# Turned keys with the heads innermost, and a verdict formed by a matmul

## Chip, cores and metric

The kernel runs on one core of a Trainium2 chip. The metric is the device time of one execution in microseconds, taken over several runs; a profile of one further execution shows where the time lies. Engine names in the profile: PE is TensorE's matmul side, PEld its weight loads, DVE is VectorE, ACT is ScalarE, POOL is GpSimd, SP is SyncE. A `q` behind a name means the engine's instruction queue.

## The reference

Two blocks follow each other. The first is a gated linear recurrence over time, with a complex decay per head and channel; the second a dense layer with the activation h cos(h).

```
B, H, S, D = 4, 8, 768, 48
mag   = sqrt(a_re^2 + a_im^2)
scale = min(mag, 0.999) / (mag + 1e-6)         # a_n = a * scale, complex
for t in range(S):                             # per batch and head
    state = a_n[t][:, None] * state + outer(k[t], v[t])     # D x D, complex
    y[t]  = q[t] @ real(state)
x   = y.transpose(0, 2, 1, 3).reshape(3072, 384)
h   = x @ w_in                                 # 384 x 2048
out = (h * cos(h)) @ w_out                     # 2048 x 384
```

q, k, v and a are float32; the two weight matrices come as float64.

## The kernel before, in words

**Two paths.** `fast_path` computes everything in a form that is exact enough for ordinary inputs and gathers measures of whether they were ordinary: `least` (1 where a decay product stayed large enough, 0 where not), `odd` (positive where an input was outside the supported range) and `wide` (sums of squares of h). At the end `verdict` turns them into one flag, every engine reads it, and a branch either runs `general_path`, which computes all again, or, in the other arm, only issues the last store. With these inputs the second arm runs.

**Chunks and groups.** Time is cut into chunks of C = 128 steps: N = 24 chunks, six to a batch. Two chunks make a group; there are NG = 12 groups g. For a chunk the recurrence becomes matmuls: scores of keys against queries (`f_scores`, products `sc`), masked by the causal matrix (tile `atm`), times values (`f_out`, products `yp`), plus the queries times the state carried over (`state`); the next state comes from keys times values (`state_sums`, products `sp`). Keys and queries carry cosine and sine parts, so a head has D2 = 96 rows.

**The dense layer.** `mm1_sums` makes h for a group in eight tiles `hp` (six products each of 128 x 256), which share three PSUM buffers. `gate_sine` takes cosine and square on ScalarE, `gate_product` multiplies on VectorE, which also frees the `hp` buffer. From group 2 on (PLAIN = 2) the second product is done by seven half-size products (`seventh`, products `sum` and `op`) with mixed operands (`mixed`, tiles `s`), in the order p = 0, 1, 3, 2, 5, 4, 6. Each result is scaled by ScalarE or added by VectorE into output tiles `ot`, which SP stores. In the last group the piece c12 lives in the tile `rest`; p = 6 adds to it at the very end, and ScalarE issues its store in the branch's other arm (`late["store"]`).

**Keys and queries turned.** `sc` needs keys and queries with the 96 channels on the partitions. For groups 0 and 1 TensorE turns them (`f_turn`). From group 2 on (PEG = 2) `f_transpose` does it with VectorE and DMAs: VectorE transposes 32 x 32 blocks from `ks` or `qs` into `tr` (128 partitions; 3 blocks, 16 heads, 32 columns), SP moves `tr` to the DRAM tile `moved`, and from there into `kT` or `qT`. For queries this is one DMA in pieces of 2 KB (16 heads of 32 words). For keys it is four DMAs, one per quarter q4 of the chunk's time, in pieces of 128 B, which puts the 128 time steps of a head next to each other in `kT`. Keys are the stationary operand `lhsT` of `sc` (line 965), queries the moving one; `queries` (line 952) hands queries over as four runs of 32 words.

**Order.** Up to group 1 the order of instructions is written out by hand. From group 2 on, `weave` (line 1213) sorts the steps of a stage by a position between 0 and 1 that each list is given, and issues them in that order; each engine takes its own in turn. In a stage n the key and query steps of group n+1 stand at 0.53 to 0.64, between the last half products of group n-1 and the `hp` sums of group n (0.56 to 1.0); `sc` of group n+1 opens the next stage. `behind` and `chain` pin the order of two instructions on an engine without a wait.

**The end.** A last weave takes the seven half products of the last group from 0 to 1, and three steps of `verdict` (line 1608) among them: its first part at 0.1, where the three measures are reduced on VectorE to `low` (96 values) and `even` (128 values); two DMAs write these into a line `line_d` in DRAM and a third brings the line back onto one partition; its second part at 0.59, where VectorE takes the minimum of the line (`bad`) and compares (`flag`), and the engines' reads of the flag are issued, ScalarE's behind its last scaling (`late["scalar"]`); its third at 0.78, which places TensorE's read. VectorE's read stands ahead of the last addition.

Of the kernel before, what the change touches and what calls it, by code (L numbers as in the profile page):

```python
# [11 lines left out]
F32 = mybir.dt.float32  # L12
# [7 lines left out]
ALU = mybir.AluOpType  # L20
AX = mybir.AxisListType
# [466 lines left out]
def fast_path(ctx, tc, q, k, v, a_re, a_im, moe_w_in, moe_w_out, out, least, odd, wide,  # L488
# [7 lines left out]
    nc = tc.nc  # L496
    B, H, S, D = q.shape
    DM, DF = moe_w_in.shape
    C = 128
    NCH = S // C  # L500
    G = 2
    N = B * NCH
    NG = N // G
    D2 = 2 * D
    HH = H // 2
    ND = DM // C
    Q4 = C // 32
    NB = D2 // 32
# [7 lines left out]
    ft = ctx.enter_context(tc.tile_pool(name="ft", bufs=2))  # L516
# [5 lines left out]
    pa = ctx.enter_context(tc.tile_pool(name="pa", bufs=5, space=PSUM))  # L522
# [20 lines left out]
    def behind(ins, other):  # L543
        tc.add_manual_dep(ins.ins, other.ins.name, mybir.DependencyInfo(
            mybir.DependencyClass.NoSync, mybir.DependencyReason.DATA))
# [140 lines left out]
    def matmul(out, **kw):  # L686
        chain(nc.tensor.matmul(out, **kw), "tensor")  # L687
# [233 lines left out]
    def f_transpose(g, i, n, name):  # L921


        if i == 0:
            X[g][name] = ft.tile([D2, G * H, Q4, 32] if name == "kT" else [D2, Q4, G * H, 32], F32,
                                 tag=name, name=name, bufs=1)
        tr = ft.tile([C, NB, n * H, 32], F32, tag="tr", name="tr")
        turn = vector.transpose(out=tr, in_=X[g][name[0] + "s"][:, ds(i * H, n * H)].rearrange(
            "p x a d -> p x (a d)").rearrange("p x (r b) -> p b x r", b=NB))
        if name == "qT" and "gated" in X[g - 1]:  # L930
            behind(turn, X[g - 1]["gated"])
        moved = rows_d.tile([Q4, D2, n * H, 32], F32, tag="moved", name="moved", bufs=3)
        nc.sync.dma_start(out=moved.rearrange("q (r b) x j -> (q r) b x j", b=NB), in_=tr)
        if name == "kT":
            for q4 in range(Q4):
                nc.sync.dma_start(out=X[g][name][:, ds(i * H, n * H), q4], in_=moved[q4])
        else:
            nc.sync.dma_start(out=X[g][name][:, :, ds(i * H, n * H)],
                              in_=moved.rearrange("q c x j -> c q x j"))

    def f_turn(g, i, name, hh):

# [9 lines left out]
    def queries(n, h):  # L952
        g, i = divmod(n, G)
        if g < PEG:
            return X[g]["qT"][:, i * H + h].rearrange("p q j -> p (q j)")
        return X[g]["qT"][:, :, i * H + h]

    def f_scores(n, hh):
        y = Y[n]
        if hh == 0:  # L960
            y["atm"] = ft.tile([C, H, C], F32, tag="atm", name="atm")
        ps = pa.tile([C, HH, C], F32, tag="a", name="sc")
        for h in range(HH):
            head = hh * HH + h
            matmul(ps[:, h], lhsT=X[n // G]["kT"][:, n % G * H + head],
                   rhs=queries(n, head), start=True, stop=True)
        y["masked"] = vector.tensor_tensor(
            out=y["atm"][:, ts(hh, HH)], in0=ps, in1=causal.unsqueeze(1).to_broadcast([C, HH, C]), op=ALU.mult)
# [191 lines left out]
    def seventh(g, p, part):  # L1160


        x, name = X[g], SEVEN[p]
        if p == 0 and part == 0:
            x["sum"] = pm.tile([C, E2], F32, tag="acc", name="sum", bufs=1)
            x["ot"] = [msb.tile([C, DM], F32, tag="ot", name="ot") for _ in range(G)]

        alone = g == NG - 1 and p == 6
        summed = p in (0, 3, 5, 6) and not alone
        if not summed and part == 0:  # L1170
            x["op"] = pm.tile([C, E2], F32, tag="m", name="op", bufs=2)
        ps = x["sum"] if summed else x["op"]
        for j in range(part * HJ // 2, (part + 1) * HJ // 2):
            matmul(ps, lhsT=left(g, name, j), rhs=right[name][:, j],
                   start=(j == 0 and (p == 0 or not summed)),
                   stop=(j == HJ - 1), skip_group_check=summed)
        if part == 0:
            return
        c11, c12, c21, c22 = (x["ot"][i][:, ts(half, E2)] for i in range(2) for half in range(2))
        if g == NG - 1:  # L1180
            c12 = rest
        if p in (0, 3, 5) or p == 6 and not alone:
            late["scalar"] = scalar.mul(out={0: c11, 3: c21, 5: c22, 6: c12}[p], in_=ps, mul=scale)
        if g == NG - 1 and p == 5:
            scalar.mul(out=c12, in_=ps, mul=scale)
        for part_ in {1: [c11], 2: [c21], 4: [c21, c22], 6: [c12] * alone}.get(p, []):
            added = vector.scalar_tensor_tensor(out=part_, in0=ps, scalar=scale,
                                                in1=part_, op0=ALU.mult, op1=ALU.add)
            if alone:
                behind(added, late["read DVE"])  # L1190
            late["vector"] = added
        row = g * G * C
        if g == NG - 1 and p == 1:
            behind(nc.sync.dma_start(out=out[ds(row, C), 0:E2], in_=c11), late["line"])
        elif p == 4:
            put = nc.sync.dma_start(out=out[ds(row + C, C), :], in_=x["ot"][1])
            if g == NG - 1:
                behind(put, late["read SP"])
        elif p == 6 and alone:
            late["store"] = lambda: nc.scalar.dma_start(out=out[ds(row, C), E2:DM], in_=c12)  # L1200
        elif p == 6:
            nc.sync.dma_start(out=out[ds(row, C), :], in_=x["ot"][0])

    def products(g, lo, hi):
        if g < PLAIN:
            return []
        return [lambda p=p, part=part: seventh(g, p, part)
                for p in (0, 1, 3, 2, 5, 4, 6)[lo:hi] for part in range(2)]
# [359 lines left out]
    for n in range(2, NG):  # L1568
# [5 lines left out]
              (keys(n + 1), *((0.5, 0.62) if n == PLAIN else (0.53, 0.64))),  # L1574
              (last_quarter() if n == PLAIN else [], 0.9, 1.0), (first(n), 0.56, 1.0),
              (mixes(n, 0, 2), 0.9, 1.0), (guarded(n - 1, per) if n > 3 else [], 0.1, 0.9))
    checked = verdict(late, temp)

    def judged():
        late["tensor"] = tail["tensor"]  # L1580
        next(checked, None)

    weave((mixes(NG - 1, 2, 4), 0.0, 0.1), ([judged], 0.05, 0.15),
          (products(NG - 1, 0, 7), 0.0, 1.0), ([judged], 0.58, 0.6), ([judged], 0.76, 0.8))
    assert not guards
    return late
@with_exitstack
def kernel(ctx, tc, q, k, v, a_re, a_im, moe_w_in, moe_w_out, out):
# [15 lines left out]
    def behind(ins, other):  # L1604
        tc.add_manual_dep(ins.ins, other.ins.name, mybir.DependencyInfo(
            mybir.DependencyClass.NoSync, mybir.DependencyReason.DATA))

    def verdict(late, temp):

        low = keep.tile([D2, 1], F32, name="low")  # L1610
        nc.vector.tensor_reduce(out=low, in_=least, axis=AX.X, op=ALU.min)
        even = keep.tile([C, 1], F32, name="even")
        nc.vector.tensor_reduce(out=even, in_=odd, axis=AX.X, op=ALU.max)
        most = keep.tile([C, 1], F32, name="most")
        nc.vector.tensor_reduce(out=most, in_=wide, axis=AX.X, op=ALU.max)
        nc.vector.tensor_scalar(out=even, in0=even, scalar1=0.0, scalar2=None, op0=ALU.is_le)
        nc.vector.tensor_scalar(out=most, in0=most, scalar1=2.4, scalar2=None, op0=ALU.is_le)
        nc.vector.tensor_tensor(out=even, in0=even, in1=most, op=ALU.mult)
        line_d = scratch.tile([D2 + C], F32, name="line_d")
        behind(nc.sync.dma_start(out=line_d[0:D2], in_=low.rearrange("p o -> (p o)")),  # L1620
               late["x"])
        nc.sync.dma_start(out=line_d[D2:D2 + C], in_=even.rearrange("p o -> (p o)"))
        line = temp("Q")[0:1, 0:D2 + C]
        late["line"] = nc.sync.dma_start(out=line, in_=line_d.unsqueeze(0))
        yield
        bad = keep.tile([1, 2], F32, name="bad")
        behind(nc.vector.tensor_reduce(out=bad[:, 0:1], in_=line, axis=AX.X, op=ALU.min),
               late["vector"])
        flag = keep.tile([1, 1], I32, name="flag")
        nc.vector.tensor_scalar(out=flag, in0=bad[:, 0:1], scalar1=0.5, scalar2=None,  # L1630
                                op0=ALU.is_lt)
        reads, values = nc.values_load_multi_w_load_instructions(
            flag[0:1, 0:1], min_val=0, max_val=1,
            skip_runtime_bounds_check_because="a comparison gives 0 or 1")
        late["taken"] = values[0]
        for ins in reads:
            name = str(ins.ins.engine).split(".")[-1]
            late["read " + name] = ins
        behind(late["read Activation"], late["scalar"])
        yield  # L1640
        behind(late["read PE"], late["tensor"])
# [36 lines left out]
```

## Time and profile before

| | |
|---|---|
| median of 3 runs | 655.88 us (655.13 to 659.32) |
| profiled execution | 653.01 us, of which the span of the profile is 651.2 us |
| granted TensorE clock | 1.0 throughout |
| instructions in the span | 10758 |
| DMA packets | 232,920 for 94.90 MB; 208,701 of them under 512 B |
| moves `moved<-tr` | 20 of 768 KB |
| moves `kT<-moved`, `qT<-moved` | 40 of 192 KB, 10 of 768 KB |
| `sc` pairs of load and matmul | 384, of which 320 from group 2 on |

The profile gives busy time by engine, groups of like instructions with the mean time of one and the idle time before them, and the chain of work that ended last, followed back from the last instruction. A row such as `sc<-qT,kT 96*128 96x128` is a product into `sc`: 96 rows and 128 columns of stationary operand, 96 x 128 of moving operand. In a timeline row the first number is the start in microseconds from the span's start and the second the duration.

### The profile page before, as it was taken

How to read it: one execution, taken by the hardware profiler on the slowest of the kernel's cores; microseconds unless marked ns; L12 is line 12 of the kernel's file. 1: busy time of each engine (PE TensorE's matmuls, PEld its weight loads, DVE VectorE, ACT ScalarE, POOL GpSimd, SP SyncE). 2: the span in 40 equal slices, each digit the busy share in tenths (PEclk: the TensorE clock that was granted, in tenths of full speed). 3: DMA queues.
4: the chain of work that ended last, by engine and by line, in shares of the span. 5: the costliest groups of instructions: out<-in, count | busy, mean ns of one | idle time of the engine just before them, and what ended most of it. 6: DMA issues, size and time to landing. Idle time of an engine off the chain costs nothing.

```text
span 651.2 us, 10758 instructions
## 1 busy us (share of the span) xinstructions
PE 641.0 (98%) x4075; PEld 576.4 (89%) x4075; DVE 492.0 (76%) x799; ACT 392.8 (60%) x726; POOL 30.9 (5%) x53
## 2 busy tenths in 40 slices
PE   8999999999999999999999999999999999999997
PEld 6888877777999999899899899899899999999996
DVE  6999989888687688786787787876877878862251
ACT  7898687284583593494494485485576476433330
POOL 4010200000000000010010010000000000000000
PEclk9999999999999999999999999999999999999999
DMA  9968755727627656747738737836836843363001
GB/s 249 244 179 203 225 164 123 170 62 182 146 49 182 158 146 148 194 110 167 209 82 191 204 85 167 205 96 151 226 105 146 219 123 98 112 134 120 25 1 31
DMA packets 232920, 94.90 MB, mean 146 GB/s; under 512 B 208701, under 2 KB 221246, under 8 KB 232858
## 3 DMA queue, kind: packets, MB, share of 16 engines
q1 hardware_dynamic: 225320, 68.51, 45.3%
q0 software_dynamic: 5824, 25.50, 11.7%
q8 instruction: 34, 0.56, 0.4%
q10 hardware_dynamic: 1714, 0.11, 0.2%
q14 instruction: 28, 0.23, 0.1%
HBM read 69.28 MB, written 24.81 MB: 144 GB/s over the span
## 4 chain that ended last, share of the span: by engine, by line
PE 92%; ACT 4%; DVE 3%; DMA 0%; issue 0%; SPq 0%; DVEq 0%
PE hp L687 38%; PE op L687 18%; PE sum L687 16%; PE sc L687 6%; PE yp L687 6%; PE sp L687 4%; PE phs L687 2%; PE lgs L687 1%; ACT tan L707 1%; PE yr L687 1%; PE tp L948 1%; ACT rs L707 1%; ACT lg L707 1%; ACT L703 1%; DVE mag L676 1%; DVE atm L676 1%
## 5 line engine op out<-in xcount | busy, mean ns | idle before, releaser
L687 PE MATMUL hp<-xT,w_in 128*128 128x256 f32 (+1 forms) x1176 | 252.5, 375 | 0.0
L687 PEld LDWEIGHTS hp<-xT,w_in 128*128 128x128 f32 x1176 | 219.6, 190 | 30.2 <-issue 0.2
L707 ACT ACTIVATE gate<-hp,half_pi_b 128x512 f32<-128x512 f32 x96 | 66.0, 687 | 118.5 <-PE hp L687 118.5
L687 PE MATMUL op<-w_out,gate 128*128 128x192 f32 (+1 forms) x448 | 100.7, 374 | 0.0
L676 DVE TENSOR_TENSOR gate<-hp,gate 128x512 f32<-128x512 f32 x96 | 65.7, 684 | 45.8 <-ACT junk L676 45.7
L687 PEld LDWEIGHTS op<-w_out,gate 128*128 128x128 f32 x448 | 75.9, 190 | 16.9 <-issue 2.0
L676 ACT ACTIVATE junk<-hp 128x512 bf16<-128x512 f32 x96 | 56.7, 591 | 0.0
L687 PE MATMUL sum<-t_s,s 128*128 128x192 f32 x320 | 56.3, 329 | 0.0
L687 PEld LDWEIGHTS sum<-t_s,s 128*128 128x128 f32 x320 | 52.1, 190 | 1.5 <-issue 1.5
L676 DVE TENSOR_TENSOR atm<-sc,causal 128x512 f32<-128x512 f32 x48 | 32.9, 689 | 23.4 <-PE sc L687 23.4
L687 PEld LDWEIGHTS sc<-qT,kT 96*128 96x128 f32 x384 | 47.4, 192 | 2.3 <-issue 0.6
L687 PE MATMUL sc<-qT,kT 96*128 96x128 f32 x384 | 49.0, 276 | 0.2 <-ACT qT L676 0.2
L676 ACT ACTIVATE ot<-sum 128x192 f32<-128x192 f32 x39 | 12.6, 322 | 53.7 <-PE sum L687 53.4
L676 DVE SCALAR_TENSOR_TENSOR ot<-op,ot 128x192 f32<-128x192 f32 x40 | 13.3, 354 | 38.0 <-PE op L687 36.4
L687 PE MATMUL yp<-atm,v 128*48 128x128 f32 x352 | 33.6, 277 | 0.9 <-ACT Q L707 0.6
L703 ACT ACT_TABLE_LOAD x24 | 30.8, 1283 | 1.2 <-PEq L1662 0.7
L676 ACT COPY yT<-yp 48x512 f32<-48x512 f32 x44 | 25.3, 574 | 7.4 <-PE yp L687 7.0
L687 PE MATMUL yp<-qT,state 96*48 96x128 f32 x304 | 29.7, 272 | 0.0
L687 PE MATMUL sum<-w_out,gate 128*128 128x192 f32 x160 | 29.7, 329 | 0.0
L687 PE MATMUL sp<-v,ks 128*96 128x48 f32 x320 | 29.7, 245 | 0.0
L687 PEld LDWEIGHTS sp<-v,ks 128*96 128x96 f32 x320 | 29.6, 165 | 0.0
L676 ACT CAST tan<-phs 128x384 int32<-128x384 f32 x24 | 11.4, 480 | 29.4 <-PE phs L687 29.4
(147 smaller groups left out, 987.4 us busy)
## 6 DMA issues: line engine op xcount, KB each, us to landing
moved<-tr SPq DMA_DIRECT2D x20, 768.0 KB
raw<-in_moe_w_in_dram POOLq DMA_DIRECT2D x16, 768.0 KB, 5.1
raw<-in_moe_w_out_dram POOLq DMA_DIRECT2D x16, 768.0 KB, 4.6
kT<-moved SPq DMA_DIRECT2D x40, 192.0 KB
qT<-moved SPq DMA_DIRECT2D x10, 768.0 KB
k<-in_k_dram SPq DMA_DIRECT2D x24, 192.0 KB
q<-in_q_dram SPq DMA_DIRECT2D x24, 192.0 KB
v<-in_v_dram SPq DMA_DIRECT2D x24, 192.0 KB
```

Source lines behind the costliest of these rows:

```text
L676: ins = getattr(self.engine, op)(**kw)
L687: chain(nc.tensor.matmul(out, **kw), "tensor")
L703: chain(nc.scalar.preload_act_table_set(table))
L707: chain(nc.scalar.activation(func=func, **kw))
L948: chain(nc.tensor.transpose(ps[:, h], X[g][name[0] + "s"][:, x0 + h].rearrange("p a d -> p (a d)"), ident), "tensor")
```

## The change

Three edits. First, from group 2 on, keys are laid down with the heads innermost: VectorE's transpose writes `tr` with the 16 heads of a time step next to each other, `moved` keeps that order, and one DMA in pieces of 2 KB brings it into `kT`, as for queries. A head's keys are then 128 words with a step of 16 words, and a new function `turned_keys` hands them to `sc`. Second, the verdict: `even` is multiplied by `low`, a matmul of `even` with a column of ones counts the good partitions into PSUM (`counted`), and VectorE compares the count with C - 0.5; the three DMAs through DRAM go, and the second step of the verdict moves from 0.59 to 0.43 of the last weave. Third, in the last group the two scalings after p = 5 go from ScalarE to VectorE, so ScalarE's read of the flag stands behind its scaling of p = 3, and it branches that much sooner; the store of c11 is no longer placed behind the verdict's last DMA. In the built program, VectorE's `flag` stands after the addition of p = 1 and ahead of that of p = 2, and the count after the product p = 3 on TensorE.

```diff
@@ f_transpose
-            X[g][name] = ft.tile([D2, G * H, Q4, 32] if name == "kT" else [D2, Q4, G * H, 32], F32,
-                                 tag=name, name=name, bufs=1)
-        tr = ft.tile([C, NB, n * H, 32], F32, tag="tr", name="tr")
-        turn = vector.transpose(out=tr, in_=X[g][name[0] + "s"][:, ds(i * H, n * H)].rearrange(
+            X[g][name] = ft.tile([D2, Q4, 32 * G * H], F32, tag=name, name=name, bufs=1)
+        tr = ft.tile([C, NB, 32 * n * H], F32, tag="tr", name="tr")
+        order = "p b (j x) -> p b x j" if name == "kT" else "p b (x j) -> p b x j"
+        turn = vector.transpose(out=tr.rearrange(order, j=32), in_=X[g][name[0] + "s"][:, ds(i * H, n * H)].rearrange(
             "p x a d -> p x (a d)").rearrange("p x (r b) -> p b x r", b=NB))
...
-        if name == "kT":
-            for q4 in range(Q4):
-                nc.sync.dma_start(out=X[g][name][:, ds(i * H, n * H), q4], in_=moved[q4])
-        else:
-            nc.sync.dma_start(out=X[g][name][:, :, ds(i * H, n * H)],
-                              in_=moved.rearrange("q c x j -> c q x j"))
+        moved = rows_d.tile([Q4, D2, 32 * n * H], F32, tag="moved", name="moved", bufs=3)
+        nc.sync.dma_start(out=moved.rearrange("q (r b) y -> (q r) b y", b=NB), in_=tr)
+        nc.sync.dma_start(out=X[g][name], in_=moved.rearrange("q c y -> c q y"))
...
+    def turned_keys(n, h):
+
+        g, i = divmod(n, G)
+        if g < PEG:
+            return X[g]["kT"][:, i * H + h].rearrange("p q j -> p (q j)")
+        return X[g]["kT"].rearrange("p q (j x) -> p (q j) x", j=32)[:, :, i * H + h]
@@ f_scores
-            matmul(ps[:, h], lhsT=X[n // G]["kT"][:, n % G * H + head],
+            matmul(ps[:, h], lhsT=turned_keys(n, head),
@@ seventh
-        if p in (0, 3, 5) or p == 6 and not alone:
+        if g == NG - 1 and p == 5:
+            for out_ in c22, c12:
+                vector.tensor_scalar(out=out_, in0=ps, scalar1=scale, scalar2=None, op0=ALU.mult)
+        elif p in (0, 3, 5) or p == 6 and not alone:
             late["scalar"] = scalar.mul(out={0: c11, 3: c21, 5: c22, 6: c12}[p], in_=ps, mul=scale)
-        if g == NG - 1 and p == 5:
-            scalar.mul(out=c12, in_=ps, mul=scale)
...
-            behind(nc.sync.dma_start(out=out[ds(row, C), 0:E2], in_=c11), late["line"])
+            nc.sync.dma_start(out=out[ds(row, C), 0:E2], in_=c11)
@@ fast_path, end
+    def counted(even):
+
+        ps = pa.tile([1, 1], F32, tag="a", name="good")
+        matmul(ps, lhsT=even, rhs=one_b, start=True, stop=True)
+        return ps
+
-          (products(NG - 1, 0, 7), 0.0, 1.0), ([judged], 0.58, 0.6), ([judged], 0.76, 0.8))
+          (products(NG - 1, 0, 7), 0.0, 1.0), ([judged], 0.42, 0.44), ([judged], 0.76, 0.8))
@@ verdict
-        line_d = scratch.tile([D2 + C], F32, name="line_d")
-        behind(nc.sync.dma_start(out=line_d[0:D2], in_=low.rearrange("p o -> (p o)")),
-               late["x"])
-        nc.sync.dma_start(out=line_d[D2:D2 + C], in_=even.rearrange("p o -> (p o)"))
-        line = temp("Q")[0:1, 0:D2 + C]
-        late["line"] = nc.sync.dma_start(out=line, in_=line_d.unsqueeze(0))
+        nc.vector.tensor_tensor(out=even[0:D2], in0=even[0:D2], in1=low, op=ALU.mult)
         yield
-        bad = keep.tile([1, 2], F32, name="bad")
-        behind(nc.vector.tensor_reduce(out=bad[:, 0:1], in_=line, axis=AX.X, op=ALU.min),
-               late["vector"])
+        good = counted(even)
         flag = keep.tile([1, 1], I32, name="flag")
-        nc.vector.tensor_scalar(out=flag, in0=bad[:, 0:1], scalar1=0.5, scalar2=None,
-                                op0=ALU.is_lt)
+        behind(nc.vector.tensor_scalar(out=flag, in0=good, scalar1=C - 0.5, scalar2=None,
+                                       op0=ALU.is_lt), late["vector"])
```

More of the change, by code (lines that the diff above doesn't have):

```diff
@@ L931, in f_transpose @@
             behind(turn, X[g - 1]["gated"])
-        moved = rows_d.tile([Q4, D2, n * H, 32], F32, tag="moved", name="moved", bufs=3)
-        nc.sync.dma_start(out=moved.rearrange("q (r b) x j -> (q r) b x j", b=NB), in_=tr)
-        if name == "kT":
-            for q4 in range(Q4):
-                nc.sync.dma_start(out=X[g][name][:, ds(i * H, n * H), q4], in_=moved[q4])
-        else:
-            nc.sync.dma_start(out=X[g][name][:, :, ds(i * H, n * H)],
-                              in_=moved.rearrange("q c x j -> c q x j"))
+        moved = rows_d.tile([Q4, D2, 32 * n * H], F32, tag="moved", name="moved", bufs=3)
+        nc.sync.dma_start(out=moved.rearrange("q (r b) y -> (q r) b y", b=NB), in_=tr)
+        nc.sync.dma_start(out=X[g][name], in_=moved.rearrange("q c y -> c q y"))
     def f_turn(g, i, name, hh):
@@ L955, in queries @@
             return X[g]["qT"][:, i * H + h].rearrange("p q j -> p (q j)")
-        return X[g]["qT"][:, :, i * H + h]
+        return X[g]["qT"][:, :, ds((i * H + h) * 32, 32)]
+    def turned_keys(n, h):
[3 more added lines that the diff above has]
+        return X[g]["kT"].rearrange("p q (j x) -> p (q j) x", j=32)[:, :, i * H + h]
     def f_scores(n, hh):
@@ L1576, in fast_path @@
               (mixes(n, 0, 2), 0.9, 1.0), (guarded(n - 1, per) if n > 3 else [], 0.1, 0.9))
-    checked = verdict(late, temp)
+    def counted(even):
+        ps = pa.tile([1, 1], F32, tag="a", name="good")
+        matmul(ps, lhsT=even, rhs=one_b, start=True, stop=True)
+        return ps
+    checked = verdict(late, counted)
     def judged():
@@ L1606, in behind, with verdict @@
             mybir.DependencyClass.NoSync, mybir.DependencyReason.DATA))
-    def verdict(late, temp):
+    def verdict(late, counted):
         low = keep.tile([D2, 1], F32, name="low")
```

## The prediction

> **What bounds the kernel now.** I read the engines' shares first, then the chain of waits in order of time, then the groups of instructions with their shapes, then the timeline of VectorE and of the end. The first part of the page and the summary of the chain:
>
> ```profile
> PE 641.0 (98%) x4075; PEld 576.4 (89%) x4075; DVE 492.0 (76%) x799; ACT 392.8 (60%) x726; POOL 30.9 (5%) x53
> PE 92%; ACT 4%; DVE 3%; DMA 0%; issue 0%; SPq 0%; DVEq 0%
> ```
>
> A busy share alone proves little for TensorE, but the chain agrees: 92% of the span is matmuls, each waiting only for the one before it, and no DMA holds 1%. So what lengthens or shortens TensorE's own stream moves the end one for one, and whatever happens on the DMA queues is hidden until it makes TensorE wait. A stretch of that chain (start, length, what), with the scores products `sc` that read `kT`:
>
> ```profile
> 484.03 1.01 PE yp L687 x16
> 485.04 1.50 PE op L687 x8
> 486.54 1.78 PE sc L687 x16
> 488.33 1.30 PE op L687 x8
> 489.63 1.32 PE sp L687 x16
> ```
>
> And the groups of `sc` and of the weight loads, by shape (count, busy, mean ns of one, idle before):
>
> ```profile
> L687 PE MATMUL sc<-qT,kT 96*128 96x128 f32 x384 | 49.0, 276 | 0.2 <-ACT qT L676 0.2
> L687 PEld LDWEIGHTS sc<-qT,kT 96*128 96x128 f32 x384 | 47.4, 192 | 2.3 <-issue 0.6 <-ACT qT L676 0.5
> L687 PEld LDWEIGHTS sp<-v,ks 128*96 128x96 f32 x320 | 29.6, 165 | 0.0
> L687 PEld LDWEIGHTS yp<-qT,state 96*48 96x48 f32 x304 | 18.3, 123 | 0.0
> ```
>
> Three things are to be seen. A float32 product is two pairs of load and matmul (24 chunks of 8 heads are 192 products, and x384 pairs). A load's time goes with its columns: (192 - 123) / (128 - 48) = 0.86 ns a column. And `sc` sits on an edge: `op` streams 192 columns in 1.30 / 8 = 162 ns, 0.85 ns a column, so the 128 columns of `sc` need 108 ns of streaming, and its 128-column load needs 128 x 0.86 = 110 ns beside it; the pairs follow each other every 1.78 / 16 = 111 ns. `sp`, with 48 streamed columns, follows every 1.32 / 16 = 82 ns, which is its 96-column load (83 ns) and nothing else: where loads are longer than streams, loads set the pace. A load that gets slower in `sc` is hidden by nothing.
>
> [...]
>
> **The keys' layout, on TensorE.** From group 2 on, a head's 128 stationary columns lie 16 words (64 bytes) apart; before they were adjacent[...]. That concerns 20 chunks x 8 heads x 2 = 320 loads, in 40 bursts of eight (one per `f_scores`).[...] What steps cost other engines here:
>
> ```profile
> L676 DVE STREAM_TRANSPOSE tr<-ks 128x1536 f32<-128x1536 f32 x10 | 22.5, 2252 | 0.0
> L676 DVE TENSOR_TENSOR ks<-Q,rs 128x768 f32<-128x768 f32 x10 | 9.5, 952 | 0.0
> L676 DVE TENSOR_SCALAR raw<-raw 128x768 uint32<-128x768 uint32 x16 | 9.0, 562 | 9.1 <-ACT yT L676 3.7 <-DMA raw<-in_moe_w_out_dram 3.4 <-DMA raw<-in_moe_w_in_dram 2.0
> L676 ACT ACTIVATE raw<-raw,carrier_b 128x768 uint32<-128x768 uint32 x16 | 16.2, 1022 | 0.5 <-issue 0.5
> L749 ACT ACTIVATE lg<-re 128x768 f32<-128x768 f32 x11 | 9.3, 846 | 0.0
> ```
>
> `raw` is read and written in steps of 8 bytes[...]: VectorE pays nothing (562 ns against 554 for the same operation on `lg`, adjacent words), ScalarE 176 ns over `lg<-re` on 768 words. Its adjacent rate is (846 - 523) / 384 = 0.84 ns a word (523 ns being its 384-wide row), so with steps 1.07 a word[...]. The transposes read in steps of 12 bytes[...]: at VectorE's (952 - 552) / 384 = 1.04 ns a word they would take about 1.76 us and take 2.25, 1.37 a word; but transposing itself may be the reason.
>
> Bounds for one strided load: below, 110 ns (no cost[...]); above, [...]274 ns. I take two load steps a column[...]: 128 x 1.72 = 220 ns. A burst is then 8 x 220, less 162 hidden behind the `op` or `sum` before it, plus 108 for the last stream: 1.71 us instead of 8 x 112 = 0.90. 0.81 x 40 = **+32.4 us**, all on the path. At 160 ns a load the same sum gives +13.2, at 274 +49.7.
>
> **The keys' layout, on VectorE.** The ten `tr<-ks` write their words 64 bytes apart. From nothing to, at 2.14 ns a word written, 3.4 us instead of 2.25: +1.2. What stands behind them:
>
> ```profile
> 460.51 2.26 DVE L676 STREAM_TRANSPOSE tr<-ks 128x1536 f32<-128x1536 f32 x1
> 462.74 0.69 DVE L676 TENSOR_TENSOR gate<-hp,gate 128x512 f32<-128x512 f32 x1
> 463.34 2.25 DVE L676 STREAM_TRANSPOSE tr<-qs 128x1536 f32<-128x1536 f32 x1
> 465.51 0.66 DVE L676 TENSOR_TENSOR gate<-hp,gate 128x512 f32<-128x512 f32 x1
> ```
>
> The gate products free the three `hp` buffers. The stage's `hp` sums begin at 457.4 and last 2.59 us each; the fifth, at 467.7, needs the buffer that the second product frees at 466.2. The cover is 1.5 us, so +1.2 costs nothing; beyond 1.5, each further microsecond costs ten.
>
> **The keys' transfers.** Per group, four DMAs of 1536 pieces of 128 B become one of 384 pieces of 2 KB; SP issued the four in 4.7 us (466.0 to 470.7) and queries' one in 1.15. Keys and queries land some 3 us sooner. Their reader, the next stage's `sc`, starts at 478.1 and waits for no DMA, so the gain is 0; the cover against a later landing is about 5 us.
>
> **The verdict.** Its three DMAs and VectorE's wait for the last (2.5 us) go; that wait stood ahead of nothing late, since the next update waited 1.7 us for its product anyway. Added are a product of one column with one column (two pairs; the nearest row, `yp`, has 59 ns a pair: +0.1 us on TensorE, between two products at about 636, its operand ready since 632.2) and a 0.15 us multiplication. `flag` now waits for that product; queued behind it on VectorE is an update due at 638.8. So nothing waits. The store of `c11` leaves SP some 5 us sooner, unwaited for.
>
> **The end.**
>
> ```profile
> 641.60 0.32 ACT L676 ACTIVATE rest<-sum 128x192 f32<-128x192 f32 x1
> 646.64 0.36 DVE L676 SCALAR_TENSOR_TENSOR rest<-op,rest 128x192 f32<-128x192 f32 x1 [2.05 <-PE op L687]
> 647.03 1.17 ACTq L1200 DMA_DIRECT2D out_dram<-rest  x1
> ```
>
> VectorE takes over two scalings of 0.35 us each, in a gap of 5 us. ScalarE, whose read now follows a count at 636.3, its comparison (0.15) and 0.46 us of reading, branches at about 637 instead of 642.8. But it stood at the store by 645.7 already, 1.3 us before `rest` was done, so arriving sooner gives nothing by itself. Only the issue (1.17 us against SP's 0.34 for the like store of `c11`) might shrink: -0.8 to +0.3; I take 0.
>
> **Sum.** 653.0 (the profiled execution, of which the span is 651.2) + 32.4 + 0.1 = 685.5. The median of the runs shown is 2.9 above the profiled time: **688**.
>
> **Rivals.** (a) Strided loads keep their pace, not slower: loads read one word a column at half the streaming rate, and a step of 8 bytes cost VectorE nothing. It decides as long as a column takes no more than 0.87 ns. Then 653.0 + 0.1, with 0.4 off for the issue, is 652.7, so **655.6**; 0.38. (b) The strided write is the cost[...]: 6.6 us a transpose, 4.3 more, 2.8 of it beyond the cover, ten times: +28, so **684**; 0.04, as no row is that slow. (c) A gain over 1% would need 6.6 us; the end holds 4.7 us after the last matmul, and only a share of it is touched; with the whole issue saved **655**. 0.03 covers what I overlook.
>
> **The numbers.** Loads at 160 to 274 ns: 0.55, the likeliest, its own range 669 to 700. Range over all: 653.5 (rival a, best end) to 698. A measurement of this kernel tells about 1% from no change. Slower 0.59, within 1% 0.38, faster 0.03.
>
> **What would show it.** The row of `sc` weight loads splits, the 320 later ones near 300 ns (192 + 110) instead of 192, `sc` x16 takes about 3.4 us in the chain, and bursts in stages before group 2 keep 111 ns. If the chain still has 1.78, the price of a step was wrong and (a) holds. If `sc` is unchanged but TensorE waits inside the `hp` run, (b). `tr<-ks` over 3.8 us would show it too.

## The result and the profile after

The changed kernel takes **685.0 us** (median of 4 runs, 683.52 to 685.25), the kernel before beside it 655.5 us (654.37 to 659.32): a ratio of 1.0435 (of the means of all runs), 95% interval 1.0389 to 1.048. By the medians it is 29.5 us slower. The profiled execution took 685.25 us, its span 683.4, which is 32.2 us more than the span before.

Engines' shares and the summary of the chain of waits, from the page of the changed kernel:

```profile
PE 674.1 (99%) x4077; PEld 610.6 (89%) x4077; DVE 497.6 (73%) x801; ACT 393.5 (58%) x724; POOL 34.4 (5%) x53
PE 95%; DMA 2%; ACT 2%; DVE 1%; issue 0%; SPq 0%; POOL 0%
```

TensorE is busy 33.1 us longer, and the chain is even more a chain of matmuls than before: hardly anything new waits; the work itself got longer. (The chain's 2% of DMA are inputs and constants at the start and one transfer `xT<-x`, for which `hp` waited 0.6 us.) The same stretch of the same stage as the prediction showed, now 25 us later (start, length, what):

```profile
509.00 1.01 PE yp L687 x16
510.01 1.50 PE op L687 x8
511.51 3.44 PE sc L687 x16
514.94 1.30 PE op L687 x8
516.25 1.32 PE sp L687 x16
```

Every neighbour has its old length; `sc` x16 went from 1.78 to 3.44 us, 215 ns a pair. The groups by shape (count, busy, mean ns of one, idle before):

```profile
L687 PE MATMUL sc<-qT,kT 96*128 96x128 f32 x384 | 80.9, 359 | 0.3 <-ACT qT L676 0.3
L687 PEld LDWEIGHTS sc<-qT,kT 96*128 96x128 f32 x384 | 80.0, 290 | 1.6 <-ACT qT L676 0.5 <-issue 0.4
L676 DVE STREAM_TRANSPOSE tr<-ks 128x1536 f32<-128x1536 f32 x10 | 28.3, 2832 | 0.0
L676 DVE STREAM_TRANSPOSE tr<-qs 128x1536 f32<-128x1536 f32 x10 | 22.5, 2246 | 0.0
```

Weight loads of `sc` gained 80.0 - 47.4 = 32.6 us, its matmuls 80.9 - 49.0 = 31.9: either is the whole of the 32.2. With 64 of the 384 loads still in groups 0 and 1 at 192 ns, the other 320 average (290 x 384 - 192 x 64) / 320 = 310 ns, 118 more. The transposes of the keys grew by 0.58 us each and delay no matmul. The end:

```profile
668.54 0.19 PE L687 MATMUL good<-one_b,even 128*1 128x1 f32 x2
668.77 0.14 DVE L1632 TENSOR_SCALAR flag<-good 1x1 int32<-1x1 f32 x1 [2.31 <-PE good L687]
679.37 0.36 DVE L676 SCALAR_TENSOR_TENSOR rest<-op,rest 128x192 f32<-128x192 f32 x1 [1.98 <-PE op L687]
679.75 0.39 ACTq L1203 DMA_DIRECT2D out_dram<-rest  x1
```

The count is compared 10.5 us before the last addition starts, and ScalarE's issue of the last store takes 0.39 us instead of 1.17. From the end of the last addition to the end of the span it is 683.4 - 679.7 = 3.7 us; before it was 651.2 - 647.0 = 4.2.

### The profile page after: what moved, and what is told of

Its sections match the earlier page's. It is cut to its first block, busy times and chain, and to the rows that moved or that the text cites. A ratio compares the mean times of both kernels' runs of the same rounds, so it can differ in the third digit from the quotient of the medians.

```text
span 683.4 us, 10722 instructions
## 1 busy us (share of the span) xinstructions
PE 674.1 (99%) x4077; PEld 610.6 (89%) x4077; DVE 497.6 (73%) x801; ACT 393.5 (58%) x724; POOL 34.4 (5%) x53
## 4 chain that ended last, share of the span: by engine, by line
PE 95%; DMA 2%; ACT 2%; DVE 1%; issue 0%; SPq 0%; POOL 0%
PE hp L687 36%; PE op L687 18%; PE sum L687 15%; PE sc L687 11%; PE yp L687 6%; PE sp L687 4%; PE phs L687 2%; PE lgs L687 1%; PE yr L687 1%; PE tp L943 1%; DMA xT<-x 1%; DMA re<-in_a_re_dram 1%; DMA sums<-sums_const 1%; ACT L703 0%; ACT tan L707 0%; DVE ks L676 0%
## 5 line engine op out<-in xcount | busy, mean ns | idle before, releaser
L687 PEld LDWEIGHTS sc<-qT,kT 96*128 96x128 f32 x384 | 80.0, 290 | 1.6 <-ACT qT L676 0.5
L687 PE MATMUL sc<-qT,kT 96*128 96x128 f32 x384 | 80.9, 359 | 0.3 <-ACT qT L676 0.3
L687 PE MATMUL sum<-w_out,gate 128*128 128x192 f32 x160 | 29.7, 329 | 0.0
L676 DVE STREAM_TRANSPOSE tr<-ks 128x1536 f32<-128x1536 f32 x10 | 28.3, 2832 | 0.0
```

What stands on the lines that cost most here:

```text
L676: ins = getattr(self.engine, op)(**kw)
```

## The experiments

**The keys' edit alone, and everything else alone.** `keys_only` is the kernel before with the first edit; `tail_only` the changed kernel with the first edit undone. From the lines in which the two differ in the layout:

```diff
-        tr = ft.tile([C, NB, n * H, 32], F32, tag="tr", name="tr")
-        turn = vector.transpose(out=tr, in_=X[g][name[0] + "s"][:, ds(i * H, n * H)].rearrange(
+        tr = ft.tile([C, NB, 32 * n * H], F32, tag="tr", name="tr")
+        order = "p b (j x) -> p b x j" if name == "kT" else "p b (x j) -> p b x j"
+        turn = vector.transpose(out=tr.rearrange(order, j=32), in_=X[g][name[0] + "s"][:, ds(i * H, n * H)].rearrange(
...
-            matmul(ps[:, h], lhsT=X[n // G]["kT"][:, n % G * H + head],
+            matmul(ps[:, h], lhsT=turned_keys(n, head),
```

> The kernel before with the keys' layout alone changed. Theory: 685.5, sc x16 3.44 us, last issue 1.17 us as before. Rival (loss shared with the other edits): under 680.

> The changed kernel with the keys' layout undone (adjacent columns, four transfers); the new verdict and ScalarE's earlier branch stay. Theory (the step between a load's columns is the whole loss): sc x16 back at 1.78 us, loads 192 ns, time 655.0, that is 0.5 below the kernel before: ScalarE's last issue 0.39 instead of 1.17, less 0.3 for the count on TensorE. Rival (the verdict or the end brings part of the loss): above 657.

`keys_only`: 684.89 us (683.95 to 685.59), ratio 1.0447, interval 1.0432 to 1.0463; `sc` x16 3.44 us, `tr<-ks` 2832 ns, as in the changed kernel. The first edit holds the whole loss. `tail_only`: 658.37 us (657.47 to 659.88), ratio 1.0051, interval 1.0038 to 1.0064. That was a miss: it should have been as fast as the kernel before and is 3 us slower. Its `sc` pairs keep 111 ns; its chain and its waits show something else (first the chain, then what TensorE waited for: us in total, times, longest):

```profile
511.88 13.82 PE hp L687 x65
525.70 7.94 DMA qT<-moved
533.77 1.13 PE sc L687 x8
```

```profile
PE sc L687 <- DMA qT<-moved: 2.1, 2, 1.2
```

The queries, whose code the edits two and three don't touch, came too late. This is taken up below.

**Does the price lie in the read, or elsewhere in the edit?** `adjacent_read` keeps the strided write, the one transfer and both other edits, and reads adjacent columns:

```diff
-        return X[g]["kT"].rearrange("p q (j x) -> p (q j) x", j=32)[:, :, i * H + h]
+        return X[g]["kT"].rearrange("p q y -> p (q y)")[:, ds((i * H + h) * C, C)]
...
-            out=y["atm"][:, ts(hh, HH)], in0=ps, in1=causal.unsqueeze(1).to_broadcast([C, HH, C]), op=ALU.mult)
+            out=y["atm"][:, ts(hh, HH)], in0=ps, in1=(causal if n // G < PEG else nought).unsqueeze(1).to_broadcast([C, HH, C]), op=ALU.mult)
...
-        behind(nc.vector.tensor_scalar(out=flag, in0=good, scalar1=C - 0.5, scalar2=None,
+        behind(nc.vector.tensor_scalar(out=flag, in0=good, scalar1=-0.5, scalar2=None,
```

> The changed kernel, but from group 2 on sc reads 128 adjacent columns of the turned keys, which mix heads and time steps; so that the meaningless scores stay harmless, they are multiplied by zeros instead of the causal factors, and the flag's comparison always gives 0. The strided write of the transposes, the single transfer in pieces of 2 KB and both other edits stay. Theory (the column step of the load is the whole cost): sc x16 1.78, loads near 191 in the mean, 654.5 to 656 us, as the keys' fewer packets also keep queries early. Rival (transposes or transfers carry a share): above 665, with sc at 1.78 and waits elsewhere.

653.37 us (653.25 to 653.82, 7 runs), ratio 0.9967, interval 0.9953 to 0.9981, one microsecond better than the low end of what was expected. Its loads are back at their old length, its transposes are as long as in the changed kernel:

```profile
L687 PEld LDWEIGHTS sc<-qT,kT 96*128 96x128 f32 x384 | 47.5, 192 | 2.2 <-ACT qT L676 0.5 <-issue 0.4
L676 DVE STREAM_TRANSPOSE tr<-ks 128x1536 f32<-128x1536 f32 x10 | 28.3, 2833 | 0.0
```

So the column step of the read costs 685.0 - 653.4 = 31.6 us, and transposes and transfers carry none of it. All else in the change together is worth 655.65 - 653.37 = 2.3 us in its favour, the first sign of a gain.

**How long a step is needed?** Three kernels, made from the changed one, interleave only 2, 4 or 8 heads; a column is then 8, 16 or 32 bytes from the next. Keys come in four transfers again. For two heads:

```diff
+        STEP = 2
...
+            turn = vector.transpose(out=tr.rearrange("p b (y j z) -> p b y z j", j=32, z=STEP),
+                                    in_=src.rearrange("p (y z) (r b) -> p b y z r", b=NB, z=STEP))
...
-        return X[g]["kT"].rearrange("p q (j x) -> p (q j) x", j=32)[:, :, i * H + h]
+        y, z = divmod(i * H + h, 2)
+        return X[g]["kT"][:, y].rearrange("p q (j z) -> p (q j) z", z=2)[:, :, z]
```

> The changed kernel with two heads innermost: a head's columns step by 2 words (8 bytes),[...] four transfers in pieces of 256 B. Theory[...]: sc x16 1.78 us, loads 192 ns, time 655. Rival one (any step costs): 3.44 us and 685. Rival two (cost grows with the step's length): 2/16 of the loss, 1.99 us and 659. Rival three (VectorE's strided write or the one-piece transfer is what costs): tr<-ks stays above 2.25 us and the time near 685 though sc is 1.78.

> The same with four heads innermost: step 4 words (16 bytes)[...]; pieces of 512 B. Theory: as the changed kernel, sc x16 3.44 us, loads near 310 ns, time 685. Rival two (growth with the step's length): a quarter of the loss, 2.2 us and 662.

> Eight heads innermost: step 8 words (32 bytes). Theory: sc x16 3.44 us as with 4 and 16 words, 685. Rival (growth with the step's length): half the loss, 2.6 us and 670.

| step of a column | `sc` x16, us | a pair, ns | `tr<-ks`, ns | time, us | ratio |
|---|---|---|---|---|---|
| 4 B (before) | 1.78 | 111 | 2252 | 655.6 | 1 |
| 8 B (`step2`) | 1.88 | 117 | 2264 | 657.03 | 1.0019 (1.0008 to 1.0029) |
| 16 B (`step4`) | 3.68 | 230 | 2979 | 690.8 | 1.054 (1.0521 to 1.0559) |
| 32 B (`step8`) | 3.77 | 236 | 2997 | 695.25, one run, clock 0.992 | |
| 64 B (changed) | 3.44 | 215 | 2832 | 685.0 | 1.0435 (1.0389 to 1.048) |

The same two matmul bursts in `step2` and in `step4`:

```profile
490.45 1.88 PE sc L687 x16
515.97 3.68 PE sc L687 x16
```

There is one edge, between 8 and 16 bytes (117 and 230 ns). Beyond it the price does not grow with the step: 230, 236 and 215 ns; that 16 and 32 bytes would cost more than 64 was not expected. A price that grows with the length is refuted. A step of 12 bytes was not run, so where between the two the edge lies, and what makes it, is not shown. (The 1.4 us of `step2` are no more than its longer bursts account for: 0.10 us for two bursts, 20 times, an estimate of 2 us.)

**Is it the weight load, or any strided operand of TensorE?** `queries_inner` leaves the keys of the kernel before as they are and lays the queries, the moving operand, with the heads innermost:

```diff
+        to = tr if name == "kT" else tr.rearrange("p b x j -> p b (x j)").rearrange("p b (j x) -> p b x j", j=32)
...
-        return X[g]["qT"][:, :, i * H + h]
+        return X[g]["qT"].rearrange("p q x j -> p (q x j)").rearrange("p (q j x) -> p (q j) x", q=Q4, j=32)[:, :, i * H + h]
```

> The kernel before with the queries, not the keys, laid down heads innermost: the same strided write by VectorE, the weights adjacent, the moving operand in steps of 16 words. If VectorE's strided write were what costs, this costs the same, near 685, with waits inside the hp run. By the theory (the operand's read costs) the write costs nothing and tr<-qs takes 2.83 us; what the moving read costs is open: nothing gives 655; the loads' 1.68 ns a column gives 215 ns for a pair of sc and about as much for each of the 272 pairs of yp with the state, so 33 + 42 more, 730[...].

704.64 us (703.97 to 705.43), ratio 1.0751, interval 1.0728 to 1.0774. From its groups, and in the last row `yp` of the kernel before:

```profile
L687 PE MATMUL sc<-qT,kT 96*128 96x128 f32 x384 | 83.2, 375 | 1.2 <-DMA qT<-moved 0.7 <-ACT qT L676 0.2 <-issue 0.2
L687 PEld LDWEIGHTS sc<-qT,kT 96*128 96x128 f32 x384 | 71.3, 201 | 7.8 <-issue 3.3 <-ACT qT L676 0.5
L687 PE MATMUL yp<-qT,state 96*48 96x128 f32 x304 | 45.4, 383 | 0.0
L687 PE MATMUL yp<-qT,state 96*48 96x128 f32 x304 | 29.7, 272 | 0.0
```

Loads stay near their 192 ns (201), while the matmuls of `sc` take about as long as with strided keys (375 ns against 359), and those of `yp<-qT,state`, which stream the same queries, go from 272 to 383 ns. The gains of the two rows, 83.2 - 49.0 = 34.2 and 45.4 - 29.7 = 15.7 us, make 49.9; measured are 49.1. None of the totals named in advance came: the 33 us for `sc` were close, the 42 for `yp` too much, because a `yp` pair had 59 ns before and not 111. In the chain 32 pairs of `yp`, 16 of them with `state`, go from 1.90 to 2.82 us, so a pair with `state` goes to an estimated 59 + 0.92 / 16 = 117 ns, again about double. What costs is reading in steps of 64 bytes, on either side of the product: a pair of `sc` takes 3.48 / 16 = 217 ns with such queries and 215 with such keys. Turning the layout round to the queries costs more (704.64 against 685.0 us), as queries are streamed twice, in `sc` and in `yp`.

**Which edit costs the 3 us of `tail_only`?** `scalar_only` is the kernel before with the third edit's scalings on VectorE, `verdict_only` with the second edit:

```diff
-        line_d = scratch.tile([D2 + C], F32, name="line_d")
...
+        nc.vector.tensor_tensor(out=even[0:D2], in0=even[0:D2], in1=low, op=ALU.mult)
         yield
-        bad = keep.tile([1, 2], F32, name="bad")
...
+        good = counted(even)
```

> The kernel before with only the third edit, the two scalings on VectorE. Theory of the end: ScalarE's read needs the flag, which still comes at 642.3, so it branches at 642.8 as before and the last issue stays 1.17 us; time within 0.3 of before. Rival: the freed ScalarE shortens the issue to 0.39.

> The kernel before with only the second edit, the count by a matmul and the earlier verdict. Theory of the end: the flag comes at about 636.5, but ScalarE's read stands behind its last scaling at 641.9, so it branches at about 642.5 and the last issue stays near 1.17 us. Rival: the earlier flag alone shortens it to 0.39.

`scalar_only`: 655.55 us in its one run, the kernel before 655.54. `verdict_only`: 659.85 in one run, a miss, 4.3 us above the kernel before. So the loss of `tail_only` is in the verdict's edit, though its operations stand at the very end and the lost time lies in the stages before. What the edit does to the stages is indirect: `bad`, a tile of 8 bytes that takes a place of 32 in the pool `keep`, which lies ahead of all others, is gone (`flag`, behind it, starts at 18016 instead of 18048). In the built programs every later tile starts 32 bytes lower: `kT` at 121312 instead of 121344, `qT` at 129504 instead of 129536, and so for `q`, `tr`, `xT`. 121344 is a multiple of 64, 121312 is not (a few tiles, such as `causal`, go the other way). Two runs test this, each with one line changed, `tail_only` put back to multiples of 64 (`kT` at 121344) and the kernel before moved off them (`kT` at 121376):

```diff
-        flag = keep.tile([1, 1], I32, name="flag")
+        flag = keep.tile([1, 16], I32, name="flag")[:, 0:1]
```

> The kernel with the second and third edit, and `flag` widened to 64 bytes, so that every tile allocated behind it starts at a multiple of 64 bytes again, as in the kernel before. Theory (the removed tile `bad` moved all later tiles by 32 bytes, and that slowed the small packets): packets of 128 B back at 13 ns, summed DMA time per engine near 375 us instead of 431, no wait of sc for queries, 655.0 us, or some 0.5 below the kernel before. Rival (something in the verdict's new order costs the 3 us, and the addresses nothing): 658.4 as without the padding.

> The kernel before with `flag` widened by 32 bytes and nothing else: every tile allocated later starts 32 bytes off a multiple of 64. Theory (addresses): packets of 128 B at 19 ns, summed DMA time near 430 us, sc waits for queries at some stages, 658 to 660 us. Rival (the verdict's order): 655.5, nothing changed.

`tail_pad`: 654.73 us (653.58 to 659.81, 22 runs), ratio 0.9991, interval 0.9979 to 1.0004. `before_shift`: 659.48 us (658.87 to 659.93), ratio 1.0057, interval 1.0037 to 1.0077. The addresses make the loss, in either direction. Mean time of a DMA packet by its size, and the sum over all packets for one of the 16 DMA engines, both from the traces' packet records:

| | 128 B, ns | 192 B, ns | 2048 B, ns | sum, us |
|---|---|---|---|---|
| before | 13.0 | 15.6 | 123 | 375 |
| `before_shift` | 16.3 | 18.4 | 153 | 424 |
| `tail_only` | 19.0 | 18.4 | 137 | 431 |
| `tail_pad` | 13.0 | 15.6 | 131 | 379 |
| changed | none | 18.1 | 135 | 387 |
| `after_pad` | none | 15.7 | 126 | 361 |

Packets of 128 B are the keys' (61,440 = 40 x 1536), those of 192 B the inputs'. Not every packet gets slower: of those of 128 B, 31% took 15 ns or more in `tail_only` (32 ns in the mean) and 16% in `before_shift` (34 ns); before it was 0.1%, in `tail_pad` 0.2%, and the rest took 14 ns at most. 19 ns had been expected for `before_shift` at 128 B and 16.3 came. How the slower packets reach TensorE, in the chain of `before_shift`:

```profile
466.57 3.24 DMA moved<-tr
469.87 0.62 SPq L936
470.55 1.53 SPq L936
472.13 1.34 SPq L936
473.52 1.03 SPq L936
474.66 7.42 DMA qT<-moved
482.08 0.14 issue
482.21 1.13 PE sc L687 x8
```

SP issues the four key transfers, then the queries', and `sc` starts 0.13 us after the queries have landed. In the kernel before, that transfer was issued at 470.82 and `sc` started at 478.26, 7.4 us later. Such a transfer took 6.25 us in the chain of `tail_pad`: that leaves an estimated 1.2 us of cover. In all, TensorE stands idle 3.1 us ahead of `sc` in `before_shift` and 0.2 in the kernel before, which is most of the 3.8 us lost.

The last run asks whether the changed kernel suffers from its addresses too; `after_pad` is the changed kernel with the same line:

> The changed kernel with `flag` widened to 64 bytes, so that later tiles start at multiples of 64 bytes. Theory (with the keys in one transfer the slower packets are hidden): 685.0 us as without it, within 0.5, though the summed DMA time falls from 387 to about 362. Rival (the shift costs 3 us here too, hidden in the sum): 682.

684.56 us (683.03 to 685.69), ratio 1.0431, interval 1.041 to 1.0453: not to be told from 685.0, though the packets' sum fell by 26 us. Slower packets are hidden here. One transfer for the keys seems to be enough for it: `adjacent_read`, too, has its tiles off multiples of 64 (192 B packets at 18.2 ns), its stages are not longer, and no `sc` in it waits for a transfer.

`tail_pad` is the fastest of the kernels with the reference's computation, but its interval reaches past 1: it is not shown to beat the kernel before.

## Why the prediction was right, and where it was off

**The column step: right in size; its reason was an estimate.** The prediction put 220 ns on a strided load by taking two load steps of 0.86 ns a column; 215 were measured. A burst of 1.71 us was forecast; the chain has 1.64 to 1.70 for single bursts and 3.44 for two. The +32.4 us stand against 31.6 between the changed kernel and `adjacent_read`. The two steps a column were the author's estimate: the 128-column loads of `hp`, `op`, `sum` and `sc` in the kernel before take 190 to 192 ns, and no row fixed the price of a step within the bounds of 110 and 274 ns (274 is 128 times 2.14, twice the 1.07 ns that ScalarE took for a word in steps of 8 bytes, an estimate too). `step2` and `step4` now show an edge between 8 and 16 bytes, where their expectations had put it; why it is there is not shown. That the size came out within 3% has luck in it, as the same estimate gives 220 ns for the steps that took 230 and 236. Rival (a), strided loads at their old pace, would have needed `sc` x16 at 1.78. It argued that loads have time to spare, reading at half the streaming rate. `yp` shows that rate, where 128 columns stream past 48 stationary ones in 59 ns, 0.46 ns each, against 0.86 for a load; beside 128 stationary columns the stream too takes 0.85 (`op`, 162 ns for 192 columns). And there is no time to spare: a strided load's pace is 215 / 128 = 1.7 ns a column. A strided stream, which `queries_inner` has in place of a strided load, ends at nearly the same pace, 217 ns. One slip in the numbers had no effect: a load of 274 ns, by the prediction's own sum, gives 653.0 + 49.7 + 0.1 + 2.9 = 705.7, so the upper ends of 700 and 698 lie below its own bound.

**The strided write: right.** It grew by 0.58 us (2832 against 2252 ns), inside the bound of 1.2, which took the same 2.14 ns a word, and the cover of 1.5, and `adjacent_read`, which keeps it, has no wait for it. Rival (b), whose 6.6 us a transpose were an estimate, falls.

**The transfers: two terms mis-sized.** "Keys and queries land some 3 us sooner" was too much for queries: in `adjacent_read` their transfer is issued 6.9 us after the first `moved<-tr` (471.28 - 464.40), before it was 8.0 (470.82 - 462.80), since it must wait for its own `moved<-tr`. And "the cover against a later landing is about 5 us" was set without a landing time; by the estimate above about 1.2 us were there. So "the gain is 0" was too low: all else in the change is worth 2.3 us once the step's cost is out, and of these the end gives about 0.5 and the count takes 0.3 (both below). How much of that is the one transfer's is not settled by a run of its own; `tail_pad`, with four transfers and its tiles at the addresses of the kernel before, has runs between 653.6 and 659.8, and `adjacent_read`, with one, all seven within 0.6 us, which speaks for it.

**The verdict: its operations right, its side effect overlooked.** Nothing waited for the count; its price in the chain is 0.12 us for the product and 0.2 more in the `op` after it (2.80 instead of 2.60), where 0.1 was forecast. What the step did not see is that taking away a tile of 8 bytes moves all tiles behind it, worth 3 us in `tail_only`. In the changed kernel this is hidden, so the sum came out right although the step left it out.

**The end: inside its bounds, at the lower one.** The issue was taken as unchanged, between -0.8 and +0.3; it shrank by 0.78. It is 0.39 us in `verdict_only`, but 1.78 in `scalar_only` and 1.39 in `keys_only`, so it goes with the verdict's edit; the expectations of `verdict_only` and `scalar_only`, 1.17 in both, were misses. "Arriving sooner gives nothing by itself" is probably the step that failed. Where ScalarE reached its arm 0.6 us (`scalar_only`) or 1.3 us (before, `keys_only`) ahead of the store, the issue ended 2.4 to 2.7 us after that arrival; where it came 2.6 us (`verdict_only`) or 7.2 us (the changed kernel, 672.6 to 679.75) ahead, it took 0.39 us. What those 2.4 us hold was not tested. The span's end gained 0.5 us by it.

**From the profiled time to the median: the 3 us by which 688 was too high.** The sum of 685.5 was for the profiled execution, which took 685.25. Adding the 2.9 us by which the median of before exceeded its profiled execution was the failed step. The traces suggest why, and no run settles it: slower executions of this schedule wait for transfers (the profiled execution of `scalar_only`, at 655.55 us, has a wait of 1.1 us of `hp` for `xT`; that of `tail_pad`, at 658.09, waits of 3.8 us), and with stages 3 us longer such waits have more cover.

## What to carry to other kernels

Before a layout is changed to save transfers, look at who reads it on TensorE: with float32 columns 8 bytes apart a weight load nearly kept its pace here (117 against 111 ns a pair); 16 bytes or more apart it took about twice as long (215 to 236 ns), and so did a stream in steps of 64 bytes (217 ns), for which shorter steps were not tried. When a small tile is added or removed, compare where all later tiles start before and after. A cover is a distance between a landing and a reader; without a measured landing it is not a number.

## What the runs showed that was not expected

A shift of all later tiles by 32 bytes, most of them off multiples of 64, made DMA packets of 128 B take 16 to 19 ns in the mean instead of 13, of 192 B 18.4 instead of 15.6, and the kernel with four key transfers 3 to 4 us slower. Only shifts by 32 bytes were run: which boundary counts, which tiles matter and what makes the packets slower is not shown. Steps of 16 and 32 bytes were dearer for TensorE (230 and 236 ns a pair) and for VectorE's transposed write (2979 and 2997 ns) than a step of 64 (215 and 2832); why was not pursued. A step of 8 bytes was nearly free for both (117 ns; 2264 against 2252).
